# The last store of a recurrence-and-MLP kernel, issued from ScalarE's queue instead of SyncE's

## The chip, the cores and the metric

One core of one Trainium2 chip. The metric is the device time of one execution in microseconds, the lower the better. All runs are of one core in the fast state (a TensorE clock of 0.998 to 1.0).

## The reference, cut to what matters

```python
# x, f_logit: (4, 6080, 256); lower_bound: (256,); w_in: (256, 2048); w_out: (2048, 256)
sig = 1.0 / (1.0 + np.exp(-f_logit))
f = lower_bound + (1.0 - lower_bound) * sig
for t in range(S):                      # a gated recurrence along the sequence
    h = f[:, t] * h + (1.0 - f[:, t]) * x[:, t]
    y[:, t] = h
x = y.reshape(24320, 256)
h = x @ w_in
out = (h - np.tanh(h)) @ w_out          # (24320, 256) float32
```

## The kernel before: the parts that matter here

Blocks of 512 tokens run through a schedule that keeps TensorE busy without a gap. The argument is only about what follows the last block. Its output is completed in two halves of 256 tokens: TensorE transposes four pieces (banks Qa, Qb, Qc, D), ScalarE and VectorE copy them to `osb`, and each half is stored by one DMA of 256 KB.

```python
        def end(j):
            ...
            for half in range(2):
                for i in range(2):
                    name = ("Qa", "Qb", "Qc", "D")[2 * half + i]
                    bank = ps_b.tile([P, KC, P], FP32, name=name, tag=name)
                    ...                                   # two transposes by TensorE
                    (nc.scalar.copy, nc.vector.tensor_copy)[i](
                        out=osb[:, 2 * half + i].rearrange("p (m k) -> p k m", k=KC),
                        in_=bank[:],
                    )
                t0 = starts[j] + half * hb
                nc.sync.dma_start(
                    out=out[t0 : t0 + hb, :].rearrange("(i p) d -> p i d", p=P),
                    in_=osb[:, 2 * half : 2 * half + 2],
                )
```

There is a guard. The fast path is valid only for small values, so a flag is computed just before (`sum_up`). At the end every engine loads it and branches around a general path, which is not taken with these inputs.

```python
    fast()
    seen = nc.values_load(flag[:].bitcast(INT32), ...)
    with tc.If(seen != 0):
        general()
```

## Time and profile before

| | before |
|---|---|
| median of the three runs first given | 2331.69 us (2330.61 to 2331.86) |
| span of the profiled run | 2328.9 us |
| VectorE's last copy ends | 2323.348 us |
| last store issued (SyncE) | 2323.641 us |
| last landing | 2327.841 us |

The profile has two parts of very unequal length. TensorE works until 2322.9 us, and after VectorE's last copy (2323.35 us) no engine computes: 5.56 us of stores, landings and final semaphores. The prediction shows the lines.

### The profile page before, as it was taken

To read this page: it belongs to the slowest core of one execution; us is meant where nothing else is said; L and a number is where in the kernel's file an instruction comes from. 1 tells how busy PE (TensorE), PEld (TensorE's weight loads), DVE (VectorE), ACT (ScalarE), POOL (GpSimd) and SP (SyncE) were. 2 spreads that over 40 slices of the span, in tenths; PEclk is the share of its full clock that TensorE was granted. 3 is DMA by queue.
4 is the path that set the end of the run, shared out by engine and by line. 5 is a ranking of instruction groups with operands and counts; after the bars stand their busy time and mean duration, and the time that the engine had idled before them with its cause. 6 is when DMAs were issued, how large, how long until landed. Compare 5 with 4: busy or idle time off the path is not lost.

```text
span 2328.9 us, 28658 instructions
## 1 busy us (share of the span) xinstructions
PE 2318.8 (100%) x10674; PEld 2024.9 (87%) x10676; DVE 2121.6 (91%) x2451; ACT 1802.2 (77%) x2688; POOL 0.7 (0%) x6
## 2 busy tenths in 40 slices
PE   9999999999999999999999999999999999999998
PEld 6888888888888888888888888888888888888887
DVE  8999899998999989999999999999899998999988
ACT  7677777777777777787777777777777777777775
POOL 0000000000000000000000000000000000000000
PEclk9999999999999999999999999999999999999999
DMA  5211211111111111112111121111211112111101
GB/s 172 64 24 32 41 37 28 28 37 37 37 28 28 38 36 37 28 28 42 32 37 28 28 45 28 37 28 28 46 29 36 28 28 46 31 34 28 28 10 28
DMA packets 296943, 85.00 MB, mean 36 GB/s; under 512 B 289888, under 2 KB 292704, under 8 KB 296800
## 3 DMA queue, kind: packets, MB, share of 16 engines
q1 hardware_dynamic: 296512, 82.87, 16.8%
q8 instruction: 84, 1.38, 0.3%
q14 instruction: 59, 0.48, 0.1%
q10 hardware_dynamic: 288, 0.26, 0.0%
HBM read 58.20 MB, written 24.90 MB: 36 GB/s over the span
## 4 chain that ended last, share of the span: by engine, by line
PE 99%; DMA 0%; SPq 0%; issue 0%; DVE 0%
PE A L392 27%; PE Qa L475 14%; PE D L392 14%; PE Qb L475 14%; PE Qd L475 14%; PE B L392 7%; PE Qc L475 7%; PE Qa L795 1%; PE Qc L795 1%; PE Qb L795 1%; PE A L728 1%; PE D L728 0%; PE Qd L728 0%; DMA xn<-in_x_dram 0%; PE B L728 0%; PE A L561 0%
## 5 line engine op out<-in xcount | busy, mean ns | idle before, releaser
L392 PE MATMUL A<-T,w_in 128*128 128x256 f32 x2208 | 558.8, 379 | 0.0
L392 PEld LDWEIGHTS A<-T,w_in 128*128 128x128 f32 x2208 | 419.5, 190 | 57.0
L436 DVE TENSOR_TENSOR h<-h,q 128x1024 f32<-128x1024 f32 x368 | 437.3, 1218 | 3.1
L430 DVE SCALAR_TENSOR_TENSOR q<-q,t 128x1024 f32<-128x1024 f32 x368 | 439.9, 1215 | 0.0
L423 ACT ACTIVATE q<-t 128x1024 f32<-128x1024 f32 x368 | 382.8, 1053 | 46.5 <-DVE h L436 43.6
L420 ACT ACTIVATE t<-h 128x1024 f32<-128x1024 f32 x368 | 388.7, 1057 | 3.1 <-DVE h L407 0.3
L441 ACT ACTIVATE junk<-t 128x1024 bf16<-128x1024 f32 x368 | 388.3, 1055 | 1.5
L455 DVE TENSOR_TENSOR Tg<-h 128x1024 f32<-128x1024 f32 x368 | 347.9, 945 | 6.3
L475 PE MATMUL Qb<-h,w_out 128*128 128x256 f32 x1472 | 347.7, 379 | 0.0
L475 PEld LDWEIGHTS Qb<-h,w_out 128*128 128x128 f32 x1472 | 279.7, 190 | 38.0
L475 PE MATMUL Qa<-Tg,w_out 128*128 128x256 f32 x736 | 219.0, 379 | 0.0
L475 PE MATMUL Qa<-h,w_out 128*128 128x256 f32 x736 | 218.9, 379 | 0.0
L475 PE MATMUL Qd<-h,w_out 128*128 128x256 f32 x732 | 217.7, 379 | 0.0
L475 PE MATMUL Qd<-Tg,w_out 128*128 128x256 f32 x732 | 217.7, 379 | 0.0
L404 ACT COPY h<-B 128x512 f32<-128x512 f32 x184 | 107.0, 582 | 142.9 <-PE B L392 94.2
L404 ACT COPY h<-A 128x512 f32<-128x512 f32 x184 | 107.1, 582 | 136.6 <-PE A L392 125.2
L407 DVE TENSOR_TENSOR h<-D,r 128x512 f32<-128x512 f32 x184 | 126.8, 689 | 93.2 <-PE D L392 89.4
L407 DVE TENSOR_TENSOR h<-A,r 128x512 f32<-128x512 f32 x184 | 126.2, 686 | 73.9 <-PE A L392 42.1
L404 ACT COPY r<-A 128x512 f32<-128x512 f32 x184 | 107.3, 583 | 105.8 <-PE A L392 105.8
L392 PE MATMUL A<-y,w_in 128*128 128x256 f32 x736 | 188.9, 379 | 0.1
L392 PE MATMUL B<-y,w_in 128*128 128x256 f32 x736 | 188.9, 379 | 0.0
L392 PE MATMUL D<-T,w_in 128*128 128x256 f32 x736 | 188.9, 379 | 0.0
(135 smaller groups left out, 3072.6 us busy)
## 6 DMA issues: line engine op xcount, KB each, us to landing
xn<-in_x_dram SPq DMA_DIRECT2D x184, 128.0 KB, 3.2
fn<-in_f_logit_dram SPq DMA_DIRECT2D x184, 128.0 KB, 3.1
out_dram<-osb SPq DMA_DIRECT2D x180, 128.0 KB, 2.8
raw<-in_moe_w_out_dram SPq DMA_DIRECT2D x8, 512.0 KB, 4.9
raw<-in_moe_w_in_dram SPq DMA_DIRECT2D x7, 512.0 KB, 5.1
out_dram<-osb SPq DMA_DIRECT2D x3, 256.0 KB, 4.1
fn<-in_f_logit_dram SPq DMA_DIRECT2D x1, 512.0 KB, 7.3
xn<-in_x_dram SPq DMA_DIRECT2D x1, 512.0 KB, 8.1
```

The source lines that it names most:

```text
L392: nc.tensor.matmul(ps[:, c], lhsT=w_in[u][:, slot, c * P : (c + 1) * P], rhs=mixes[j][right], start=start and c == 0, stop=True, skip_grou ...
L404: nc.scalar.copy(out=dst, in_=piece(n, bank))
L407: nc.vector.tensor_tensor(out=piece(n, "h")[:, q], in0=piece(n, bank), in1=piece(n, r), op=ALU.add)
L420: nc.scalar.activation(out=half(n, i, "t"), in_=half(n, i), func=AF.Square)
L423: nc.scalar.activation(out=half(n, i, "q"), in_=half(n, i, "t"), func=AF.Square, scale=RA, bias=RB,)
L430: nc.vector.scalar_tensor_tensor(out=q, in0=q, scalar=RC, in1=t, op0=ALU.add, op1=ALU.mult)
L436: nc.vector.tensor_tensor(out=h, in0=h, in1=q, op=ALU.mult)
L441: nc.scalar.activation(out=junk[:, :, :, 0 : st[n]["hb"]], in_=t, func=AF.Relu, bias=-TINY, accum_out=flags[:, 2 * n + i : 2 * n + i + 1],)
L455: nc.vector.tensor_tensor(out=o, in0=a, in1=b, op=ALU.subtract)
L475: nc.tensor.matmul(acc[j, part][:, r, 0 : st[n]["hb"]], lhsT=w_out[u][:, slot, c * P : (c + 1) * P], rhs=piece(n, right)[:, q, c], start=( ...
L728: nc.tensor.matmul(h[c], lhsT=w_in[u][:, 2 * k + s, c * P : (c + 1) * P], rhs=ys[j][:, k, 0:nb], start=k == 0 and (c == 0 or len(banks) == 2),
L795: nc.tensor.matmul(acc[j][i // 2][:, i % 2].rearrange("p (k m) -> p k m", k=2), lhsT=plain[j, u][:, s, c, i * P : (i + 1) * P], rhs=w_out[ ...
```

## The change

Half 1's store waits behind half 0's in SyncE's order. ScalarE can start DMAs too and has nothing left to do, so the intent is that the second issue need not wait for the first.

```diff
                 t0 = starts[j] + half * hb
-                nc.sync.dma_start(
+                (nc.sync, nc.scalar)[half].dma_start(
                     out=out[t0 : t0 + hb, :].rearrange("(i p) d -> p i d", p=P),
                     in_=osb[:, 2 * half : 2 * half + 2],
                 )
```

## The prediction

> **What bounds the kernel now.** I began with the page's totals and its chain of waits. The time to beat is 2331.69 us, the median of three runs (2330.61 to 2331.86, so 1.25 us apart). TensorE is busy for the whole span, and the chain that ended last is 99% TensorE.
>
> ```profile
> span 2328.9 us, 28658 instructions
> ## 1 busy us (share of the span) xinstructions
> PE 2318.8 (100%) x10674; PEld 2024.9 (87%) x10676; DVE 2121.6 (91%) x2451; ACT 1802.2 (77%) x2688; POOL 0.7 (0%) x6
> ...
> PE 99%; DMA 0%; SPq 0%; issue 0%; DVE 0%
> ```
>
> The change touches nothing in that body: it concerns only the last two stores, after TensorE has finished. So I read the timeline from 2322 us to the end.
>
> ```profile
> 2322.12 0.39 ACT L581 COPY osb<-Qa 128x256 f32<-128x256 f32 x1 [2.04 <-PE Qa L578]
> ...
> 2322.34 0.42 DVE L581 COPY osb<-Qb 128x256 f32<-128x256 f32 x1
> ...
> 2322.70 0.38 ACT L581 COPY osb<-Qc 128x256 f32<-128x256 f32 x1 [0.19 <-PE Qc L578]
> 2322.92 0.42 DVE L581 COPY osb<-D 128x256 f32<-128x256 f32 x1 [0.16 <-PE D L578]
> 2323.13 0.91 SPq L586 DMA_DIRECT2D out_dram<-osb  x2
> ```
>
> Columns are start, duration, engine and line. Half 0 (Qa, Qb) is complete at 2322.34 + 0.42 = 2322.76 us, half 1 (Qc, D) at 2322.92 + 0.42 = 2323.34. Both stores go through SyncE. The trace's own records put the first issue at 2323.131 for 395 ns and the second at 2323.641 for 397 ns. So half 1 waits 0.30 us, data ready, for SyncE. That 0.30 us is all that the change can go for at the source. The same line's summary gives issue lengths and landing times.
>
> ```profile
> L586 SPq DMA_DIRECT2D out_dram<-osb x2: 395/396/397, 2323.1 to 2323.6; - x2
> ...
> DMA to landing us min/median/max: 4.1/4.1/4.2
> ```
>
> From 2323.64 to the end of the span is 5.26 us, and nothing computes in it: 4.2 us to landing and 1.03 us of final drains and semaphores (last landing 2327.841, last record 2328.9). Next I ask what SyncE waits for there. In the view of waits of its queue, the end line is L1113.
>
> ```profile
> SPq L1113 <- DMA out_dram<-osb: 2.2, 2, 1.6
> ```
>
> Columns are total us, times, longest. It waits twice for landings, 1.6 us and then about 0.6 us more; the landings end the program. But why 4.2 us for 256 KB? The view of stretches (busy per engine, clock, DMA share, GB/s in the last two columns) tells it.
>
> ```profile
> 2324.50:2325.00 0.50, 0.00 (x0) 0.00 (x0) 0.00 (x0) 0.00 (x0) 0.00 (x0) 1.00 1.02 350
> 2325.00:2325.70 0.70, 0.00 (x0) 0.00 (x0) 0.00 (x0) 0.00 (x0) 0.00 (x0) 1.00 0.77 262
> 2325.70:2326.30 0.60, 0.00 (x0) 0.00 (x0) 0.00 (x0) 0.00 (x0) 0.00 (x0) 1.00 0.13 32
> 2326.30:2326.75 0.45, 0.00 (x0) 0.00 (x0) 0.00 (x0) 0.00 (x0) 0.00 (x0) 1.00 0.07 25
> 2326.75:2327.45 0.70, 0.00 (x0) 0.00 (x0) 0.00 (x0) 0.00 (x0) 0.00 (x0) 0.77 0.06 22
> ```
>
> Until 2325.7 all sixteen DMA engines move data; after 2326.3 the share is 0.06 to 0.07, which is one engine of sixteen. That one is late. The queues in the stretch 2324.0 to 2325.7 show what else was running.
>
> ```profile
> q1 hardware_dynamic: 495, 0.48, 83.3%
> q8 instruction: 1, 0.02, 6.1%
> q14 instruction: 1, 0.01, 1.6%
> ```
>
> The q8 packet is a 16 KB instruction fetch; the packet records give it 2324.047 to 2325.695, 1.65 us. 6.1% of sixteen engines is 0.97 of one, so one engine has it the whole stretch. Each half is 256 KB, 16 packets of 1 KB per engine. Only then come 32 more store packets of the late engine in a row: six slow ones to 2326.31, ten at a 42 ns pace and half 0's semaphore write at 2326.736, sixteen of half 1 and its write at 2327.420. Fifteen of half 0's sixteen increments are in by 2325.583, the last at 2327.206; for half 1, 2326.737 and 2327.841.
>
> **What the Trainium skill says.** "DMA: Bandwidth & Descriptors", section "Issuing engines are not separate DMA queues": stores from ScalarE and SyncE run on the same sixteen engines, and issuing from several saves only the sequencer's time. The records agree at the kernel's start, where both queues issue at 0.988 us (382 ns on ScalarE, 399 ns on SyncE) and their packets then run side by side. "Runtime: NRT & Kernel Launch", section "Instruction fetch mechanics": sequencers fetch instructions in 16 KiB blocks by a DMA queue of their own, and a taken branch breaks the sequential prefetch. The 16 KB packet fits; TensorE's branch at 2322.937 is its likely cause, which nothing here proves. "Perfetto Trace Analysis", section "DMA Instruction — HWDGE (DVE, Sync)": the issue's recorded time covers descriptor generation, with a possible wait for a lock on the generator, and not the movement. So 0.395 us stands beside a landing 4.1 us away, as measured.
>
> **The change part by part.** It removes one issue of 0.397 us from SyncE and adds one to ScalarE, which has only its own last copy before it (ends 2323.09). The program order shows ScalarE's other work unchanged, and the new store still waiting for VectorE's last copy. No instruction moves on TensorE or VectorE.
>
> - Issue of half 1: ready at 2323.34 plus some 0.03 us for the wait to pass (second issue: 30 ns from wait to issue). So it starts at about 2323.40 instead of 2323.64, 0.24 us earlier. If the generator serves one queue at a time, it must wait until 2323.526, and the gain is 0.1 us.
> - Fifteen engines: half 1 may land up to 0.24 us sooner. But these are in by 2326.74, 1.10 us before the last. No gain.
> - The late engine: it gets the same fetch, the same 16 + 16 packets, from the same start at 2324.05. Half 1's packets on it begin at 2326.742, about 2.7 us after their issue ended (2324.038). Issuing them 0.24 us earlier makes them wait longer. Two rings can mix the halves, so half 0 may land later, nearer to half 1's time; the sum of work stays, and the last landing stays at about 2327.84.
> - SyncE: its flag load, branch and early waits finish at 2325.56 now; they move 0.4 to 0.5 us forward into a wait of 1.6 us. No gain.
> - ScalarE: its flag load (467 ns) and branch came at 2322.71 to 2323.29; they now follow the issue, estimated to end at 2323.40 + 0.40 + 0.06 + 0.47 + 0.11 = 2324.44. It is next needed at 2328.1. No loss.
>
> Sum: 0.0 us on the last landing, with perhaps 0.1 to 0.2 us gained if the fetch falls elsewhere in an unprofiled run. I take 2331.5, against 2331.69.
>
> **The rivals.** (a) The issue is the path: the end follows half 1's issue, and the whole 0.24 us (or even the 0.51 us between the two issue starts) is gained: 2331.2 to 2331.45. For it: half 1 is visibly held by SyncE. Against: its packets then sit idle behind a busy engine. (b) ScalarE's later branch makes its own instruction fetch collide with the stores. Two 8 KB fetches (552 and 434 ns, q14) already fall in the tail without being last; on the late engine one would add about 0.5 us: 2332.2. Against: it would have to meet the very engine that is late. (c) ScalarE's queue, unused since the first microseconds, issues slowly, or the two queues contend for the generator: up to 0.5 us later, still within the slack of the late engine: no change. (d) The fetch finds the store packets already in line and is itself spread out; the engine's total remains, and so does the time.
>
> **Range and chances.** All outcomes lie within 0.7 us of 2331.5, 0.03% of the time; a 2% change is 46.6 us, seventy times as much. The spread of the three runs before, 1.25 us, is larger than the effect and makes the range: 2330.4 to 2332.6. Within 2%: 0.98; faster and slower 0.01 each, for a disturbed run.
>
> **What would show it.** On ScalarE's queue one issue from L586 at about 2323.4 to 2323.7 on the same clock of events; on SyncE one issue less. Again a stretch of over 1 us with DMA share 0.06, the last landing about 4.5 us after TensorE's final transposes end, and half 0's landing no earlier than before. Wrong would be a last landing over 0.2 us earlier with the fetch still in the way (then rival a), or later by 0.4 us or more with another fetch beside it (rival b).

## The result, and the profile after

Six runs each: 2330.92 us with the change (2330.52 to 2331.67), 2330.70 us before (2330.50 to 2331.86). The ratio is 1.0, with a 95% interval of 0.9987 to 1.0013: the same. A ratio here is the mean time of one kernel's fast runs over that of the other's from the same rounds, so it is not quite the ratio of the medians. The interval is about 3 us to either side, far more than the 0.24 us that the change could move. The clocked times therefore could not have shown the effect, and the argument below rests on the traces, of which there is one for each run. All outputs are right.

The timeline of the changed kernel (start, duration, engine, line) shows that the change did what it set out to do at the issue.

```profile
2322.57 0.43 DVE L581 COPY osb<-Qb 128x256 f32<-128x256 f32 x1
...
2322.93 0.38 ACT L581 COPY osb<-Qc 128x256 f32<-128x256 f32 x1 [0.19 <-PE Qc L578]
2323.15 0.42 DVE L581 COPY osb<-D 128x256 f32<-128x256 f32 x1 [0.15 <-PE D L578]
2323.36 0.39 SPq L586 DMA_DIRECT2D out_dram<-osb  x1
2323.65 0.41 ACTq L586 DMA_DIRECT2D out_dram<-osb  x1
```

ScalarE's issue begins 0.08 us after VectorE's last copy ends (2323.573), and overlaps SyncE's. Before it began 0.29 us after. So half 1 is issued 0.22 us earlier. Now the view of stretches: busy time per engine, then clock, DMA share and GB/s.

```profile
2324.50:2325.00 0.50, 0.00 (x0) 0.00 (x0) 0.00 (x0) 0.00 (x0) 0.00 (x0) 1.00 0.96 336
2325.00:2325.70 0.70, 0.00 (x0) 0.00 (x0) 0.00 (x0) 0.00 (x0) 0.00 (x0) 1.00 0.94 326
2325.70:2326.30 0.60, 0.00 (x0) 0.00 (x0) 0.00 (x0) 0.00 (x0) 0.00 (x0) 1.00 0.32 97
2326.30:2326.75 0.45, 0.00 (x0) 0.00 (x0) 0.00 (x0) 0.00 (x0) 0.00 (x0) 1.00 0.06 23
2326.75:2327.45 0.70, 0.00 (x0) 0.00 (x0) 0.00 (x0) 0.00 (x0) 0.00 (x0) 1.00 0.07 23
```

The same shape as before: all engines, then over a microsecond with a share of 0.06 to 0.07, one engine of sixteen. The queues from 2324.2 to 2325.8 us (packets, MB, share) have half 1 on its own queue, q10, and the same instruction fetch of 16 KB.

```profile
q1 hardware_dynamic: 256, 0.25, 46.4%
q10 hardware_dynamic: 232, 0.23, 40.9%
q8 instruction: 1, 0.02, 5.7%
```

And SyncE's waits at the end, in total, times and longest:

```profile
SPq L1113 <- DMA out_dram<-osb: 2.9, 1, 2.9
```

Before there were two waits for landings, 2.2 us in total. SyncE now gets to the end earlier and waits longer there, once.

Here is where the time went between the two profiles, by the trace's records, from VectorE's last copy:

| us | before | after | difference |
|---|---|---|---|
| VectorE's last copy ends, from the start of the span | 2323.348 | 2323.573 | +0.225 |
| half 1's issue starts | 0.293 | 0.077 | -0.216 |
| 16 KB instruction fetch ends | 2.347 | 2.152 | -0.195 |
| last landing | 4.493 | 4.293 | -0.200 |
| from the last landing to the end of the span | 1.067 | 1.187 | +0.120 |
| whole end, from the last copy | 5.560 | 5.480 | -0.080 |

The span grew by 0.225 - 0.080 = 0.145 us. The last landing is 0.2 us sooner, which looks like the gain in the issue, but it follows the end of the fetch by 2.14 to 2.15 us in both, and the fetch was 0.18 us shorter (1.471 against 1.648 us). The experiments below tell the two apart. The 0.120 us come from the order of SyncE's final checks. It tests one semaphore after the other, each test 0.06 us. Before, half 1's semaphore was followed by two more tests, and the build now gives half 1 another one with four behind it.

### The profile page after: what moved, and what is told of

Its sections match the earlier page's. It is cut to its first block, busy times and chain, and to the rows that moved or that the text cites. A ratio compares the mean times of both kernels' runs of the same rounds, so it can differ in the third digit from the quotient of the medians.

```text
span 2329.1 us, 28660 instructions
## 1 busy us (share of the span) xinstructions
PE 2319.0 (100%) x10676; PEld 2024.9 (87%) x10676; DVE 2122.1 (91%) x2451; ACT 1802.1 (77%) x2688; POOL 0.7 (0%) x6
## 3 DMA queue, kind: packets, MB, share of 16 engines
q8 instruction: 84, 1.38, 0.3%
## 4 chain that ended last, share of the span: by engine, by line
PE 99%; DMA 0%; SPq 0%; issue 0%; DVE 0%
PE A L392 27%; PE Qa L475 14%; PE D L392 14%; PE Qb L475 14%; PE Qd L475 14%; PE B L392 7%; PE Qc L475 7%; PE Qa L795 1%; PE Qc L795 1%; PE Qb L795 1%; PE A L728 1%; PE D L728 0%; PE Qd L728 0%; DMA xn<-in_x_dram 0%; PE B L728 0%; PE A L561 0%
```

## The experiments

Twelve runs were made, of eleven kernels. My theory: one DMA engine, held by TensorE's 16 KB instruction fetch, ends last, and half 1's issue is not on the path. The rivals: the issue is the path; or that engine is slow by itself. This table has the ends of all runs, in us from VectorE's last copy. In copies_by_half that is a different copy, so its figures stand apart. The fetch is taken to be TensorE's from an estimate: 84 packets of 16 KB on q8 are 1.38 MB for 10,674 matmuls and 10,676 weight loads, 64.5 bytes each, and no other engine has over 3,500 records.

| run | half 1 issued | fetch ends | last landing | end |
|---|---|---|---|---|
| before | 0.293 | 2.347 | 4.493 | 5.560 |
| after | 0.077 | 2.152 | 4.293 | 5.480 |
| noguard_sp | 0.297 | none | 2.859 | 3.814 |
| noguard_act | 0.076 | none | 2.744 | 3.831 |
| noguard_copy4 | 1.019 | none | 3.197 | 4.284 |
| copy4 | 1.018 | 1.980 | 4.057 | 5.245 |
| copy9 | 3.088 | 2.097 | 5.273 | 6.538 |
| swap | 0.366 | 2.459 | 4.156 | 5.223 |
| one_store | 0.366 | 1.774 | 4.066 | 5.195 |
| pe12 | 0.077 | 2.279 | 4.420 | 5.608 |
| late_flag_act | 0.076 | 4.236 | 2.861 | 4.500 |
| late_flag_sp | 0.438 | 3.982 | 2.987 | 4.053 |
| late_flag_sp2 | 0.437 | 3.699 | 3.030 | 4.097 |
| copies_by_half | 0.450 | 2.936 | 5.073 | 6.260 |

**noguard_sp: both stores from SyncE, without the guard.**

```diff
     fast()
-    seen = nc.values_load(flag[:].bitcast(INT32), ...)
-    with tc.If(seen != 0):
-        general()
```

> The kernel before without its final flag check (flag load, branch, general path); both stores from SyncE. My theory: one DMA engine ends last because TensorE's 16 KB instruction fetch holds it. If the taken branch causes that fetch, it is gone here, no stretch with the DMA share of one engine follows, the last landing comes about 1.2 to 1.6 us sooner after VectorE's last copy starts (4.9 us before), and the time falls by 1 to 2 us. If the fetch is only the next in a steady row of them (one every 28 us), it stays and the time falls by less than 0.3 us. Rival 'this engine is slow by itself': the late engine stays without a fetch beside it.

The stretches of noguard_sp, with the last copy ending at 2322.545 us, and its queues from 2322.70 us on:

```profile
2323.70:2324.20 0.50, 0.00 (x0) 0.00 (x0) 0.00 (x0) 0.00 (x0) 0.00 (x0) 1.00 1.04 363
2324.20:2324.70 0.50, 0.00 (x0) 0.00 (x0) 0.00 (x0) 0.00 (x0) 0.00 (x0) 0.65 0.98 346
2324.70:2325.20 0.50, 0.00 (x0) 0.00 (x0) 0.00 (x0) 0.00 (x0) 0.00 (x0) 0.50 0.22 72
2325.20:2325.70 0.50, 0.00 (x0) 0.00 (x0) 0.00 (x0) 0.00 (x0) 0.00 (x0) 0.50 0.00 0
```

```profile
q1 hardware_dynamic: 544, 0.52, 27.8%
q14 instruction: 1, 0.01, 0.6%
```

The data share falls from full to nothing with no stretch of one lone engine. The q8 packet is gone (83 in the whole trace, 84 before), and the last landing is 1.63 us sooner (1.2 to 1.6 were expected). The median was 2329.39 us against 2331.19 (ratio 0.9993, interval 0.9976 to 1.001): the profile is clear, the clocked times are within their spread. The engine is not slow by itself.

**noguard_act: the same with the change.** The edit is as above, on the changed kernel.

> The changed kernel without its final flag check; against noguard_sp it has the change alone, without (if the branch causes it) the late engine. My theory after reading the traces: the sixteen engines are all busy from 2324.05 us on, so half 1 queues behind half 0 and even without the late engine the earlier issue gains at most 0.1 us in the last landing. Rival 'the issue is the path, and the fetch alone hid it': last landing 0.2 to 0.25 us sooner than in noguard_sp, measured from VectorE's last copy.

Its stretches, with the last copy ending at 2324.311 us:

```profile
2325.50:2326.00 0.50, 0.00 (x0) 0.00 (x0) 0.00 (x0) 0.00 (x0) 0.00 (x0) 1.00 0.98 342
2326.00:2326.50 0.50, 0.00 (x0) 0.00 (x0) 0.00 (x0) 0.00 (x0) 0.00 (x0) 1.00 1.00 350
2326.50:2327.00 0.50, 0.00 (x0) 0.00 (x0) 0.00 (x0) 0.00 (x0) 0.00 (x0) 1.00 0.13 41
```

This is the change alone, without a late engine. The issue is 0.221 us earlier and the last landing 0.115 us earlier, just over the 0.1 us expected. But this is the last increment alone. The trace shows a half's landing as sixteen increments of its semaphore, read here as one for each DMA engine, and the first fifteen of half 1 come at 2.511 to 2.690 us here and at 2.513 to 2.697 us in noguard_sp: no gain. Half 0's packets run until 1.64 us and half 1's first packet starts only at 1.438, 0.95 us after its issue ended (0.52 us in noguard_copy4 below, where the engines have room): it queues. Why the sixteenth lags by 0.16 us in noguard_sp and by 0.05 us here is not shown. From the last landing to the end there are 1.087 us in place of 0.955, which is 0.132 us more, for the two extra checks. The end is at 3.831 against 3.814 us. So even with the fetch out of the way, the gain, if it is the change's, is eaten by the order of the checks. The median was 2329.07 us (ratio to before 0.9988, interval 0.9971 to 1.0005).

**copy4 and noguard_copy4: half 1 made 0.94 us later, with and without the fetch.** ScalarE writes its copy of Qc four times (the same values).

```diff
-                    (nc.scalar.copy, nc.vector.tensor_copy)[i](...)
+                    for _ in range(4 if (half, i) == (1, 0) else 1):
+                        (nc.scalar.copy, nc.vector.tensor_copy)[i](...)
```

> The changed kernel with ScalarE's copy of Qc written four times in place of once (same values), so that the store of half 1 is ready about 1.0 to 1.3 us later. My theory (half 1's packets would wait 2.7 us behind the late engine's work): last landing within 0.2 us of that of the changed kernel, time unchanged. Rival 'the issue of half 1 is the path': last landing and time 1.0 to 1.3 us later.

> noguard_act with ScalarE's copy of Qc written four times, so that half 1 is issued 0.94 us later and no late engine covers it. With the late engine (copy4) the same delay cost nothing. My theory: here it shows, but not in full, since half 1 then finds the engines free: about 2.1 us from issue to landing in place of 2.7, so last landing at about 3.1 to 3.3 us after VectorE's last copy ends, against 2.74, and the end 0.35 to 0.55 us later than noguard_act's 3.83. Rival 'half 1's issue is never on the path': end unchanged. Rival 'issue-bound': end 0.94 us later.

The timeline and then the stretches of copy4, with the last copy ending at 2323.360 us:

```profile
2323.15 0.39 SPq L587 DMA_DIRECT2D out_dram<-osb  x1
2324.38 0.41 ACTq L587 DMA_DIRECT2D out_dram<-osb  x1
```

```profile
2325.05:2325.55 0.50, 0.00 (x0) 0.00 (x0) 0.00 (x0) 0.00 (x0) 0.00 (x0) 0.56 0.42 145
2325.55:2326.05 0.50, 0.00 (x0) 0.00 (x0) 0.00 (x0) 0.00 (x0) 0.00 (x0) 0.50 1.00 344
2326.05:2326.55 0.50, 0.00 (x0) 0.00 (x0) 0.00 (x0) 0.00 (x0) 0.00 (x0) 0.50 0.14 47
2326.55:2327.05 0.50, 0.00 (x0) 0.00 (x0) 0.00 (x0) 0.00 (x0) 0.00 (x0) 0.50 0.06 20
```

The engines run partly dry between the halves (0.42), and still one lone engine ends last (0.06). The issue moved by 0.94 us and the last landing did not become later: it is 0.236 us sooner (0.2 us either way was expected), again after a fetch that ended 0.172 us sooner. The median was 2331.69 us against 2331.19 (ratio 1.0001). Without the guard the same delay lengthens the end from 3.831 to 4.284 us, 0.45 us, in the middle of what was expected (0.35 to 0.55). The issue and the stretches of noguard_copy4, with the last copy ending at 2324.490 us:

```profile
2325.51 0.41 ACTq L587 DMA_DIRECT2D out_dram<-osb  x1
```

```profile
2326.20:2326.70 0.50, 0.00 (x0) 0.00 (x0) 0.00 (x0) 0.00 (x0) 0.00 (x0) 1.00 0.47 166
2326.70:2327.20 0.50, 0.00 (x0) 0.00 (x0) 0.00 (x0) 0.00 (x0) 0.00 (x0) 1.00 0.92 340
2327.20:2327.70 0.50, 0.00 (x0) 0.00 (x0) 0.00 (x0) 0.00 (x0) 0.00 (x0) 1.00 0.07 21
```

The dip is the same, but the 0.07 is now the end of all engines together: the last store packet ends at 2327.335 us, and half 1's increments all come within 0.18 us (3.015 to 3.197 on the table's clock). Its median was 2330.24 us against 2330.95 (ratio 0.9995, interval 0.9979 to 1.001), too wide to say more. This pair is the main evidence: the same delay is free with the fetch and costs 0.45 us without it.

**copy9: half 1 made 3.0 us later.** As copy4, with nine copies.

> The changed kernel with Qc written nine times, half 1 issued about 3.0 us later than in the changed kernel (0.416 us for each of 8 more copies, less what stood behind VectorE). My theory: this is more than the slack of about 1.7 us that the late engine leaves, so half 1 now decides: issue at about 3.1 us after VectorE's last copy ends, landing about 2.1 us later at 5.2, end at about 6.4 against 5.48 of the changed kernel; time about 0.9 us longer. Rival 'hidden whatever it is': end within 0.2 us. Rival 'issue-bound': 3.0 us longer.

The last landing came at 5.273 us and the end at 6.538: now half 1 is the path, as expected from the sum. The median was 2332.82 us against 2330.95 for the kernel before (1.9 us more; 0.9 over the changed kernel were expected; ratio 1.0005, interval 0.9989 to 1.002). The profile's own end is 1.06 us longer than that of the changed kernel. So the slack in half 1's issue is between 0.94 and 3.0 us.

**pe12: 12 idle matmuls after TensorE's last transposes.**

```diff
+            late = ps_a.tile([P, TB], FP32, name="A", tag="A")
+            for _ in range(12):
+                nc.tensor.matmul(late[:], lhsT=zeros.bitcast(BF16)[:, 0:P],
+                                 rhs=zeros.bitcast(BF16)[:, 0:TB], start=True, stop=True, ...)
```

> The changed kernel with 12 idle matmuls (128x512, about 0.21 us each) on TensorE after its last transposes, so that TensorE's branch comes 1 to 2.5 us later; the stores are not touched. If the branch causes the 16 KB fetch, the fetch starts 1 to 2.5 us later than the first store packet, the store packets of that engine go first, the last landing comes up to 1.2 us sooner, and the time falls by 0.5 to 1.2 us though TensorE does more. If the fetch belongs to the steady row, it comes at the same place or earlier, and the time changes by less than 0.5 us. Rival 'slow engine': no change.

This one missed its aim. TensorE's sequencer runs ahead of the array: the branch came at -0.350 us in place of -0.414, just 0.06 us later. The fetch's record starts 0.67 us later (1.351) but is shorter (0.928 us) and ends at 2.279, and the last landing again follows it by 2.14 us. Nothing follows about the cause of the fetch. One thing stays open: in this trace the late engine took none of its 32 store packets between 0.70 us, when the other engines began, and 2.27 us, although the fetch is only recorded from 1.351 us. copy9 shows the same over 0.36 us (fetch recorded from 1.066 us). The recorded start may not be the moment at which the engine is taken. The median was 2331.74 us against 2331.19 (ratio 0.9999).

**late_flag_act and late_flag_sp: the flag behind the stores.** The same instructions, with the flag's last two steps (a sum by TensorE, a copy by ScalarE) moved, so that every engine's flag load and branch come later.

```diff
-                        if final and name == "o3":
-                            sum_up()
                         if final and name == "o4":
                             end(j)
+                            sum_up()
```

> The changed kernel with the one-element reduction and copy of the flag moved behind the two stores: the same instructions, but every engine's flag load and branch come about 1.3 to 1.9 us later (TensorE's branch at about 1.0 to 1.5 us after VectorE's last copy ends, in place of 0.41 us before it). My theory (TensorE's branch calls for the 16 KB fetch, which holds one DMA engine while 32 store packets wait): the fetch now starts after that engine's store packets, the last landing falls from about 4.3 to about 2.8 us after VectorE's last copy ends, and the end of the program from 5.5 to about 3.9; time 1.2 to 1.7 us less. Rival 'the branch is not the cause, the end of TensorE's work is': fetch and last landing stay where they are. Rival 'a later flag lengthens the end itself': landing early, but the end later than 4.5 us.

> As late_flag_act, with both stores from SyncE. My theory: the change is worth about 0.1 us in the last landing here (0.115 us without the flag check) and nothing in the time, since SyncE has two more semaphore checks of 0.06 us behind the last landing when ScalarE's store is on its other semaphore. So the end within 0.1 us of late_flag_act. Rival 'the issue is the path once the fetch is out of the way': end 0.22 us later than late_flag_act.

The stretches of late_flag_sp, with the last copy ending at 2322.399 us:

```profile
2323.70:2324.20 0.50, 0.00 (x0) 0.00 (x0) 0.00 (x0) 0.00 (x0) 0.00 (x0) 1.00 1.03 361
2324.20:2324.70 0.50, 0.00 (x0) 0.00 (x0) 0.00 (x0) 0.00 (x0) 0.00 (x0) 1.00 0.92 342
2324.70:2325.20 0.50, 0.00 (x0) 0.00 (x0) 0.00 (x0) 0.00 (x0) 0.00 (x0) 1.00 0.31 105
2325.20:2325.70 0.50, 0.00 (x0) 0.00 (x0) 0.00 (x0) 0.00 (x0) 0.00 (x0) 1.00 0.13 33
```

The stores are over by 2325.1 us; what moves after that are instruction fetches, which nobody waits for. TensorE's branch moved from -0.41 to +1.31 us, the fetch from 0.70 to 2.98 (its start), and the last landing from 4.493 to 2.987. In all eleven traces that have the guard, the fetch's record starts 1.09 to 1.70 us after TensorE's branch, wherever that is. So the fetch goes with the flag check. Whether the load of the flag or the branch calls for it, these runs do not separate. TensorE's last matmul also moved, but only by 0.7 us (from -0.47 to 0.24), the fetch by 2.3. The end is at 4.053 us, 1.5 us less than before, and the median 2330.16 us against 2331.88.

With ScalarE's store (late_flag_act) I expected an end at about 3.9 us, within 0.1 us of late_flag_sp's, and that was wrong: the last landing is 0.126 us sooner (again by the sixteenth increment alone; the fifteenth comes at 2.849 and 2.844 us), but the end is at 4.500 us, 0.447 us later. The rival named there, that a later flag lengthens the end itself, is what happened. SyncE's waits in late_flag_act show why.

```profile
SPq L1112 <- remote: 0.9, 1, 0.9
...
SPq L1078 <- ACT flag L889: 0.4, 1, 0.4
```

No wait for a store is left. ScalarE's copy of the flag now stands behind its DMA issue (flag copy at 0.531 us, against 0.280 from SyncE only), and then all five engines load the flag at once, which takes 1.09 to 1.19 us. In late_flag_sp the four others took 0.64 to 0.81 and SyncE followed. SyncE passes its branch at 1.90 us and is idle until 2.87, by a wait to which the profile gives only "remote". The trace's records name it: SyncE's first final check waits for semaphores that GpSimd (POOL) sets at the end of its own way through the branch. GpSimd branches at 1.955 us, makes four semaphore checks, and at 2.755 us begins the instruction (INC_SWDGE_SEM) whose update comes at 2.852; SyncE's check follows at 2.869, 0.017 us later. In late_flag_sp the same update comes at 2.188 and the check at 2.205. The checks for the stores, after it, no longer have to wait. The flag chain, by way of GpSimd, has become the end, so here the change costs time. The median was 2330.41 us against 2331.88.

**late_flag_sp2: the same kernel again, for the time.**

> The same kernel as late_flag_sp once more, for the time: ratio to the kernel before between 0.9990 and 0.9998 (0.5 to 2.3 us less), end of the program 4.0 to 4.3 us after VectorE's last copy ends, no landing later than 3.1. If the gain of late_flag_sp was the spread of the runs, the ratio is 1.0000 or more.

The end came at 4.097 us and the last landing at 3.030. The ratio is 0.9995 (0.9982 to 1.0009), after 0.9994 (0.9981 to 1.0008) in the first series: medians 2330.31 against 2330.95 us, and 2330.16 against 2331.88. Each interval still holds 1.0. The profiles agree on an end that is 1.5 us shorter than that of either kernel; that the clocked time is lower is likely from both series and not shown beyond its spread.

**swap: half 0 from ScalarE, half 1 from SyncE.**

```diff
-                (nc.sync, nc.scalar)[half].dma_start(
+                (nc.scalar, nc.sync)[half].dma_start(
```

> The queues exchanged: half 0 from ScalarE, half 1 from SyncE. ScalarE's copy of Qc stands behind the store of half 0 in its order, so it should start only after that issue, about 0.5 us later than in the changed kernel, and half 1 is issued about 0.3 to 0.4 us later than in it. My theory: hidden, the last landing within 0.25 us of the end of the fetch plus 1.9 us, time unchanged. Rival 'the issue of half 1 is the path': end 0.3 to 0.4 us later.

The timeline of swap:

```profile
2323.96 0.41 ACTq L586 DMA_DIRECT2D out_dram<-osb  x1
2324.04 0.42 DVE L581 COPY osb<-D 128x256 f32<-128x256 f32 x1 [0.15 <-PE D L578]
2324.41 0.38 ACT L581 COPY osb<-Qc 128x256 f32<-128x256 f32 x1 [0.78 <-PE D L578]
2324.83 0.40 SPq L586 DMA_DIRECT2D out_dram<-osb  x1
```

ScalarE's copy of Qc stands behind its own DMA issue and starts 0.59 us later than in the changed kernel, so half 1 is issued 0.29 us later. In the trace 11 of half 0's 16 packets on the late engine went out before the fetch (recorded from 1.231 us) held it, and so the last landing follows the fetch's end by 1.70 us and not by 2.14 (1.9 within 0.25 was expected). The end (5.223 us) did not grow, and the median is 2331.28 us against 2331.88 (ratio 0.9999). The change put the right half on ScalarE, but the wrong one would have cost nothing either.

**one_store: a single store of 512 KB from SyncE.**

```diff
-                nc.sync.dma_start(out=out[t0 : t0 + hb, :]..., in_=osb[:, 2 * half : 2 * half + 2])
+            nc.sync.dma_start(out=out[starts[j] : starts[j] + 2 * hb, :]..., in_=osb[:, 0:4])
```

> The kernel before with one store of 512 KB from SyncE in place of two of 256 KB; it waits for all four copies, so the first packet comes about 0.3 us later than in the kernel before. My theory: the late engine has the same fetch and the same 32 packets, so the last landing stays within 0.3 us of fetch end plus 2.15 us and the time is unchanged within noise. Rival 'the start of the first half decides': last landing 0.3 us or more after that sum.

The last landing is at 4.066 us, 2.29 us after the fetch's end (expected 2.15, within 0.3), and the end at 5.195. The median is 2331.67 us against 2330.95 (ratio 1.0002). The split into halves, whose second half the change tries to speed up, is itself worth nothing as the kernel stands.

**copies_by_half: VectorE copies half 0, ScalarE half 1.**

```diff
-                    (nc.scalar.copy, nc.vector.tensor_copy)[i](
+                    (nc.vector.tensor_copy, nc.scalar.copy)[half](
```

> The changed kernel with both copies of half 0 on VectorE and both of half 1 on ScalarE, so that no store waits for two engines. In both kernels SyncE's first store starts 0.33 us after its last named wait was met and 0.034 us after ScalarE's copy of Qc, which it need not wait for. If that copy is what it waits for, the issue now follows VectorE's second copy by 0.06 us; if it is a cost of its own on SyncE after a long wait, 0.3 us or more remain. Time: unchanged either way by my theory, because the late engine decides.

SyncE's store started 0.028 us after VectorE's second copy ended, and 0.117 us before Qc's copy ended, so neither a wait for Qc nor a cost of every long wait fits. late_flag_sp rules out Qc as well: there the gap is again 0.333 us, with Qc complete 0.19 us before the issue. In the thirteen other traces, before and after included, the gap is 0.332 or 0.333 us, and in each a separate semaphore check that had to wait stands ahead of that store. In copies_by_half the store carries its one wait itself. On ScalarE such a check is followed by the issue after 0.038 us (changed kernel). What makes SyncE's 0.333 us stays open; it is not on the path. The median was 2330.98 us against 2331.88 (ratio 0.9996).

## Why the prediction was right, point by point

The forecast was 2331.5 us, 2330.4 to 2332.6, and 0.98 for "within 2%". 2330.92 us is in the range and the ratio is 1.0. The 0.6 us between forecast and result are not of the change: the six runs before have a median of 2330.70 us, 1.0 us below the median of three that I started from. The range was the spread of the runs, and all outcomes that the prediction lists, rivals included, lie in it. So the number alone tells nothing of the mechanism; that is what the points below are for.

- **The issue.** Expected 0.24 us earlier, or 0.1 us if the descriptor generator serves one queue at a time; measured 0.216 us, with both issues overlapping (SyncE -0.209 to 0.185 us, ScalarE 0.077 to 0.488). Right, and the lock did not show.
- **Fifteen engines.** "Up to 0.24 us sooner" was too high. In the changed kernel the first thirteen increments of half 1 came at 2.51 to 2.70 us, against 2.53 to 2.69 before: next to nothing. What I did not put into the sum is that half 1 queues behind half 0: in the changed kernel its first packet starts at 1.446 us, 0.96 us after its issue ended. Without the guard fifteen increments gained nothing either, and only the last one came 0.115 us sooner.
- **The late engine.** Right, and now tested: without the fetch it is gone, a delay of 0.94 us behind it costs nothing, and a moved fetch frees it. In before and after the last store packet ends 1.73 us after the fetch. That the halves might mix on two rings did not happen: half 0 landed on the late engine 1.51 us after the fetch's end in both. By the prediction's own sign it was a near thing: the last landing was to move by 0.0 us and came 0.200 us sooner with the fetch in the way, and "over 0.2" was to speak for rival (a); half 0's landing, which was to be no earlier, came 0.2 us earlier as well. Only the fetch's end (0.195 us sooner) and copy4, where a later issue goes with a sooner landing, tell that this was the fetch and not the issue.
- **TensorE's branch as the cause of the fetch.** Called likely and unproved in the prediction. noguard_sp and late_flag_sp show that the flag check is the cause. That it is the branch in it is likely still, and not shown.
- **SyncE.** Moved into its wait, as said, by 0.73 us (first check at 1.000 us, before 1.727) and not 0.4 to 0.5, since its flag load was also shorter, 0.492 against 0.720 us.
- **ScalarE.** Done at 1.41 us, where the forecast of 2324.44 us is 1.09 on this clock. Its flag load took 0.759 us in place of 0.467. No loss, as said.
- **What the sum lacked.** The order of SyncE's final checks: +0.120 us. It takes back what the landing gained without the fetch, 0.115 to 0.126 us. I had looked at the program's order, but not at which semaphore the store would get and how many checks follow it.
- **A sign that I gave wrongly.** "Last landing about 4.5 us after TensorE's final transposes end" was mis-added: by the records it was 4.96 us before and 4.75 after. The 1.03 us from the last landing to the end was 1.067.
- **The rivals.** (a), the issue as the path, falls with copy4 as the kernel stands. Without the fetch a later issue does cost (noguard_copy4, 0.45 of 0.94 us), but an earlier one gained 0.115 us of 0.221 at most. (b) did not happen: the last landing stands at the same distance from the fetch's end as before, and the one later 8 KB fetch (2.461 to 2.770 us) began when the other engines had taken all their store packets. (c) did not show, ScalarE's issue took 0.411 us against 0.397. (d) is open, since pe12 and copy9 do not tell when the engine is taken.

## What to carry to other kernels

Before you speed up the start of a last transfer, look at what its end waits for: a DMA share of 0.06 is one engine of sixteen, and if that one lags, earlier issues only lengthen its line. A flag check near the end brought an instruction fetch over the same DMA engines here, so try it where no store is in flight, and then check that the flag's own chain has not become the end. Judge an effect of 0.1 us on a clock that starts at the last common event, since the runs differ by a microsecond for other reasons.

## What the Trainium skill lacked or had wrong

- "Runtime: NRT & Kernel Launch", section "Instruction fetch mechanics", calls the cost of crossing a block boundary "mostly hidden" and, for a branch, speaks of a stall of the engine itself. The section lacks what the fetch costs the kernel's own transfers on the same DMA engine: here one 16 KB fetch kept 32 store packets of 1 KB waiting, and the last landing was 1.63 us later than without it (4.493 against 2.859 us), while TensorE itself went on at once (its drain stands 0.2 us after its branch). It gives blocks of 16 KiB for all engines; this trace has 84 fetches of 16 KB and 59 of 8 KB.
- "DMA: Bandwidth & Descriptors", section "Issuing engines are not separate DMA queues", is right here that a second issuing engine saves only issue time (0.22 us earlier; without the fetch at most 0.115 us in the last landing). That section lacks the cost at the end: the order in which SyncE tests the semaphores, 0.06 us each, made 0.120 us here. I found no page that has it.
- No page that I read tells how the time of a flag load changes when several engines load at once: 0.47 to 0.49 us on TensorE and ScalarE in the kernel before, where the starts are 0.37 us apart, and 1.09 to 1.19 us for five begun within 0.012 us in late_flag_act. Whether the loads slow each other or the stores slow them is not shown: a load in the midst of the stores took 0.720 us in the kernel before.
- "Perfetto Trace Analysis", section "DMA Instruction — HWDGE (DVE, Sync)", puts a possible wait for a lock into the recorded issue and gives no length for it. With both queues issuing at once none showed: 0.394 us on SyncE and 0.411 on ScalarE, against 0.395 and 0.397 one after the other on SyncE, and 0.410 for ScalarE's issue in copy4, where it ran alone.
